# Attention scores in pairs of steps over six PSUM banks, and a transpose moved from TensorE to SyncE

## The chip, the cores and the metric

One core of a Trainium2 chip runs the whole kernel. The metric is the device time of one execution in microseconds, as the median of three runs. Times of single instructions come from one profiled execution of the same program, which is a little shorter than the measured time (612.9 us from its first to its last instruction against 615.9 us).

The engines are TensorE (PE; its weight loads are PEld), VectorE (DVE), ScalarE (ACT), GpSimd (POOL) and SyncE (SP), which here only issues transfers. Each engine runs its own list of instructions in a fixed order, and semaphores hold an instruction until what it needs is there.

## The reference

Eight batches of eight heads, 576 rows, head dimension 64. Attention with a threshold, then a mixer of low rank over the rows, then a two-layer network with relu over the channels:

```python
scores = scale * np.matmul(q, k.transpose(0, 1, 3, 2))          # 64 heads of 576 x 576
thresh = np.max(scores, axis=-1, keepdims=True) - tau
scores = np.where(scores >= thresh, scores, -1000000000.0)
scores = scores - np.max(scores, axis=-1, keepdims=True)
attn = np.exp(scores)
attn = attn / (np.sum(attn, axis=-1, keepdims=True) + 1e-09)
x = np.matmul(attn, v)                                            # heads side by side: (8, 576, 512)

xt = x.transpose(0, 2, 1)
h = xt @ U @ V                                                    # rank 32 over the rows
u = x + h.transpose(0, 2, 1)
ch = np.maximum(u @ w_ch1, 0.0) @ w_ch2                           # 512 -> 2048 -> 512
out = u + ch
```

## The kernel before

The kernel works on head pairs: two heads at a time, 32 pairs in all, four pairs to a batch. A head pair has 4.5 tiles of 128 rows, so two head pairs make nine score steps, and the kernel has 144 of them. A score step computes 128 rows of both heads of a pair against all 576 columns. The head dimension is 64, so TensorE is used as four 64 x 64 tiles: two heads (j) and two halves of the rows (h). All other matmuls use it as one 128 x 128 array. The scores are float32.

```python
pair_bank = [psum.tile([P, 2, 512], FP32, name=f"scores{n}") for n in range(2)]   # 4 banks of PSUM
bank = [psum.tile([P, 512], FP32, name=f"bank{n}") for n in range(4)]             # the other 4

# one score step: 8 matmuls of 64 x 288
for c in range(2):
    cs = slice(c * HC, (c + 1) * HC)
    for j in range(2):
        hs = slice(64 * j, 64 * j + 64)
        for h in range(2):
            a, rows, part = pr, slice(i * P + HB * h, i * P + HB * h + HB), slice(HB * h, HB * h + HB)
            if i == 4:
                a, rows, part = two[h], slice(512, S), two[h].part4
            nc.tensor.matmul(pair_bank[j][part, c, 0:HC], a.tT[hs, 0, rows], a.tT[hs, 1, cs],
                             start=True, stop=True)
```

What follows a score step, for each of the two heads x: VectorE scales the scores out of PSUM and takes the row minimum of the negated scores ("weigh"), ScalarE makes the threshold and the exponential, VectorE selects and sums ("select"), GpSimd copies a piece of the row ("twin"), and SyncE turns the weights by a transposing transfer ("turn_w"; for some of the first pairs TensorE turns them instead, "turn_pe"). Then TensorE multiplies them with the values.

```python
nc.vector.tensor_scalar(out=s_sb.rearrange("p (a c) -> p a c", a=2), in0=pair_bank[x][:, :, 0:HC],
                        scalar1=-scale, scalar2=None, op0=ALU.mult, op1=ALU.min,
                        accum_out=m[:, x:x + 1])                                    # weigh
nc.scalar.activation(out=e_sb, in_=s_sb, func=ACT.Exp, bias=m[:, x:x + 1], scale=-1.0)
nc.vector.scalar_tensor_tensor(out=w_sb[:, 0:S], in0=s_sb, scalar=thr_[:, x:x + 1], in1=e_sb,
                               op0=ALU.is_le, op1=ALU.mult, accum_out=pr.den[:, i, x:x + 1])  # select
nc.sync.dma_start_transpose(...)                                                    # turn_w
```

Later a head pair's u (128 columns of four row tiles) is narrowed to bf16 on ScalarE, turned by four transposes on TensorE into a bank, and copied out by ScalarE:

```python
def turn_u(t):
    ps = bank[t.got[0]][:, 0:256].bitcast(BF16)
    for i in range(4):
        nc.tensor.transpose(ps[:, i * P:(i + 1) * P], pr.ub[:, i, :], identb)

deps = [ub] + (done.get(("p1", pr.b - 2), []) if pr.hp == 0 else [])
uT_ = done["uT_", p] = add(PE, 0.23, turn_u, deps, banks=1, kind="uT")

def copy_u(_):
    nc.scalar.copy(out=bt.uT[:, pr.hp, :], in_=bank[uT_.got[0]][:, 0:256].bitcast(BF16))

done["uT", p] = add(SCA, 0.53, copy_u, [uT_, got("uT", p - 1)], frees=[uT_])
```

The network's first product ("up", 16 groups of four 128x512 matmuls for a batch) is followed by a relu on ScalarE, the second ("down", four quarters of four matmuls each for a row tile) by an addition on VectorE and a store.

The order of all of this is made while the program is built. Each piece of work is a task with an engine, a guessed cost and its dependencies; a list scheduler picks, for each engine, the task with the lowest rank (the guessed time at which it is ready, plus an offset by its kind, OFF). Tasks of the network have due times in score steps (DUE). Where the scheduler expects TensorE idle for more than 0.45 us, it puts in matmuls of the identity with no use but to keep TensorE busy ("fill"). A task that writes PSUM takes the bank that has been free longest:

```python
for e in range(5):
    cands = []
    for t in ready[e]:
        s = max(at[e], t.ready)
        if t.banks:
            s = max(s, last[free[t.banks - 1]])
    ...
    s, t = min((c for c in cands if c[0] <= first + self.PATIENCE[e]), key=rank)
...
while at[PE] + 0.45 < s and last[n] <= at[PE]:
    self.filler(n)
...
t.got = free[:t.banks]
```

Of the kernel before, what the change touches and what calls it, by code (L numbers as in the profile page):

```python
# [8 lines left out]
P = 128  # L9
FP32 = mybir.dt.float32  # L10
# [9 lines left out]
HC = S // 2  # L20
HB = 64
# [3 lines left out]
SOFT = 4  # L25
EARLY = 8


W1_AT = (1, 4, 6, 9, 11, 14, 16, 19)
W2_AT = (20, 21, 23, 24, 25, 26, 28, 29)  # L30

DUE = (218.25, 193.25, 202, 58.75, 370.75, 342.5, 322.25, 741.75)

# [15 lines left out]
class Task:  # L49
    __slots__ = ("engine", "cost", "fn", "deps", "off", "banks", "frees", "lag", "kind", "when",  # L50
                 "dma", "ndma", "steps", "left", "after", "ready", "at", "end", "got")

    def __init__(self, engine, cost, fn, deps=(), banks=0, frees=(), lag=0.0, kind=None,
                 when=None, dma=0.0, ndma=1, steps=0):
        self.engine, self.cost, self.fn = engine, cost, fn
        self.deps = [d for d in deps if d is not None]
        self.banks, self.frees, self.lag, self.kind = banks, frees, lag, kind
        self.steps = steps
        self.dma = dma
        self.ndma = ndma  # L60
        self.when = when
        self.after, self.ready, self.end, self.got = [], 0.0, None, []


class Order:
# [11 lines left out]
    PARTS = {"S": "quadrants"}  # L77


    OFF = {  # L80
        "copy_main": (-65.55, 4.27, -33.19), "copy_rest": (46.32, -22.93, -32.89), "copy_tt":
        (55.52, 75.97, 78.39), "copy_u": (-9.24, 32.51, 27.95), "copy_u4": (-33.7, -103.34, 12.57),
        "copy_w": (26.76, -36.81, 20.04), "down": (9.11, -38.52, 30.41), "exponential": (-75.1,
        348.03, 34.33), "finish": (-81.29, -4.31, -38.11), "first": (-55.84, 39.98, -12.2), "high":
        (318.07, 5.62, 10.21), "inverse": (-108.97, -22.9, -67.36), "join": (10.42, -3.6, 8.15),
        "load": (-8.71, 35.51, -42.16), "low": (12.45, 36.07, 40.66), "low_part": (-39.21, 135.95,
        -5.41), "low_rank": (-33.23, -18.24, 8.92), "make": (-24.27, 38.39, 1.66), "narrow": (-16.4,
        -76.48, 195.67), "narrow_u": (60.65, 3.75, -17.1), "narrow_u4": (-18.43, 20.09, 16.7),
        "norm": (-28.14, -232.63, 8.05), "product": (124.81, 96.76, 14.8), "relu": (108.49, 92.35,
        46.18), "rest": (63.06, -59.16, 27.83), "scores": (-50.96, -12.67, -95.71), "select":  # L90
        (118.77, 57.08, 91.87), "send": (-69.4, 60.79, -21.09), "spread": (48.74, -2.19, -63.39),
        "spread4": (79.29, 25.05, 4.44), "spread_v": (11.62, 75.45, 21.95), "sum_u": (-26.95,
        -36.59, 53.52), "sum_u4": (54.92, -47.81, 31.47), "sums": (-140.25, 32.72, -84.66),
        "threshold": (-37.93, 79.1, -43.59), "turn4": (71.1, 12.6, 27.31), "turn_main": (-113.51,
        69.4, 58.93), "turn_pe": (-18.8, -21.2, 34.54), "turn_rest": (15.16, 27.93, 15.36),
        "turn_u": (-21.99, 92.75, -1.81), "turn_w": (-17.93, -115.14, 3.52), "twin": (-84.09,
        -15.28, -93.69), "up": (-7.21, -32.4, -1.5), "values": (-8.3, -68.34, -10.67), "weigh":
        (28.1, 41.88, 60.36), "weights": (8.1, -7.95, 22.31),
    }
# [4 lines left out]
    def add(self, *args, **kw):  # L104
        t = Task(*args, **kw)
        t.off = self.OFF[t.fn.__name__][self.phase]
        self.tasks.append(t)
        return t

    def run(self):  # L110
# [24 lines left out]
        while left:  # L135
            best = None
            free = sorted(range(self.nbanks), key=lambda n: last[n])
            for e in range(5):
                cands = []
                for t in ready[e]:  # L140
                    s = max(at[e], t.ready)
                    if t.banks:
                        s = max(s, last[free[t.banks - 1]])
                    if e == POOL and t.dma:
                        s = max(s, lanes[t.ndma - 1 - self.LANES])
                    if s < NEVER:
                        cands.append((s, t))
                if not cands:
                    continue
                first = min(s for s, _ in cands)  # L150
                s, t = min((c for c in cands if c[0] <= first + self.PATIENCE[e]), key=rank)
                if best is None or s < best[0]:
                    best = (s, t)
# [15 lines left out]
            left -= 1  # L169
            t.got = free[:t.banks]  # L170
            for n in t.got:
# [13 lines left out]
            for f in t.frees:  # L185
                for n in f.got:
                    last[n] = t.end + self.SIGNAL[e]
# [11 lines left out]
def kernel(  # L199
# [81 lines left out]

    pair_bank = [psum.tile([P, 2, 512], FP32, name=f"scores{n}") for n in range(2)]
    bank = [psum.tile([P, 512], FP32, name=f"bank{n}") for n in range(4)]

# [12 lines left out]
    def got(*key):  # L297
        return done.get(key)
# [73 lines left out]


    def prepare_tasks(p):
        pr = pairs[p]
        loads = load_tasks(p, pr)
# [45 lines left out]


    step = [0]
    tiles = [0]
    gate = {}

    def score_tasks(p, i):


        pr = pairs[p]
        n = step[0]
# [4 lines left out]

        def scores(_):

            for c in range(2):  # L440
                cs = slice(c * HC, (c + 1) * HC)
                for j in range(2):
                    hs = slice(64 * j, 64 * j + 64)
                    for h in range(2):
                        a, rows, part = pr, slice(i * P + HB * h, i * P + HB * h + HB), \
                            slice(HB * h, HB * h + HB)
                        if i == 4:
                            a, rows, part = two[h], slice(512, S), two[h].part4
                        nc.tensor.matmul(pair_bank[j][part, c, 0:HC], a.tT[hs, 0, rows],  # L449
                                         a.tT[hs, 1, cs], start=True, stop=True)  # L450

        deps = [got(name, p + a) for a in range(2 if i == 4 else 1)
                for name in ("qT", "kT", "qk4T")]
        deps += [got("P1", n - 1, x) for x in range(2)]
        S_ = done["S", p, i] = add(PE, 0.97, scores, deps, kind="S", steps=1)
        if i == 4:
            done["S", p + 1, 4] = S_

        mins = []
        for x in range(2):  # L460
            def weigh(_, x=x, s_sb=s_ring[(tiles[0] + x) % NS]):
                nc.vector.tensor_scalar(  # L462
                    out=s_sb.rearrange("p (a c) -> p a c", a=2), in0=pair_bank[x][:, :, 0:HC],
                    scalar1=-scale, scalar2=None, op0=ALU.mult, op1=ALU.min,
                    accum_out=m[:, x:x + 1])

            t = add(VEC, 0.69, weigh, [S_, got("w", tiles[0] + x - NS)])
            done["P1", n, x] = t
            if x == 0 and n in gate:
                for w in gate[n]:  # L470
                    w.deps.append(t)
            mins.append(t)
# [81 lines left out]

    def value_tasks(p):
        pr = pairs[p]
        bt = pr.batch
# [127 lines left out]

        def turn_u(t):

            ps = bank[t.got[0]][:, 0:256].bitcast(BF16)
            for i in range(4):
                nc.tensor.transpose(ps[:, i * P:(i + 1) * P], pr.ub[:, i, :], identb)  # L690

        deps = [ub] + (done.get(("p1", pr.b - 2), []) if pr.hp == 0 else [])
        uT_ = done["uT_", p] = add(PE, 0.23, turn_u, deps, banks=1, kind="uT")

        def copy_u(_):
            nc.scalar.copy(out=bt.uT[:, pr.hp, :], in_=bank[uT_.got[0]][:, 0:256].bitcast(BF16))

        done["uT", p] = add(SCA, 0.53, copy_u, [uT_, got("uT", p - 1)], frees=[uT_])


# [39 lines left out]

    def mixer_tasks(b):
        bt = batches[b]

# [42 lines left out]
        for i in range(NT if bt.odd else 4):  # L786
            halves = []
            for g in range(4):
# [6 lines left out]

                when = due + 134.5 if i == 4 and b < B - 1 else due + 46.5 + 13.25 * (i + g / 4) / 4
                halves.append(add(PE, 0.865, down, (relus4 if i == 4 else relus) + weights2 + (
# [80 lines left out]
    for p in range(0, NP, 2):  # L878
        order.phase = 0 if p < NPAIR else 1 if p < NP - NPAIR else 2
        prepare_tasks(p)  # L880
        prepare_tasks(p + 1)
        for i in range(NT):
            score_tasks(p, i)
        for i in range(4):
            score_tasks(p + 1, i)
        value_tasks(p)
        value_tasks(p + 1)
        if (p + 1) % NPAIR == NPAIR - 1:
            mixer_tasks(p // NPAIR)
# [37 lines left out]
```

## Time and profile before

| | |
|---|---|
| time, median of 3 | 615.9 us (615.58 to 616.2) |
| span of the profiled execution | 612.9 us |
| VectorE, select / weigh | 288 x 861 ns / 288 x 748 ns |
| ScalarE, exponential / relu of "up" | 288 x 772 ns / 144 x 592 ns |
| DMA, mean over the span | 143 GB/s; 87.35 MB |
| granted clock of TensorE | 0.999 |

How to read it: a row of a group names the line, the engine, the operation, what it writes and reads, and how often; then the busy time in us and the mean length of one in ns; then the idle time of the engine just before these instructions and what ended it. Lengths of matmuls are modelled and overlap, so the time that a matmul costs TensorE is read from the starts in the timeline. A row of waits names who waited, for whom, how long in all, how often and the longest.

### The profile page before, as it was taken

The numbers are of one execution on the slowest core, as the hardware profiler recorded it, in microseconds if no ns is written. First come the engines' busy times: TensorE is split into PE (matmuls) and PEld (weight loads), VectorE is DVE, ScalarE is ACT, GpSimd is POOL, SyncE is SP. The second block draws the span as 40 slices with busy tenths as digits, with TensorE's granted clock in tenths as the row PEclk, the third lists the DMA queues.
The fourth block names the chain that finished last, engine by engine and source line by source line (L and its number), as shares of the span: only waits on it lengthen the run. The fifth ranks groups of instructions, "written<-read, shape, count | busy, mean of one in ns | idle before, by whom it ended". The sixth has DMA issues, their size and how long they took to land.

```text
span 612.9 us, 17317 instructions
## 1 busy us (share of the span) xinstructions
PE 600.8 (98%) x6339; PEld 346.1 (56%) x6339; DVE 521.0 (85%) x1399; ACT 478.3 (78%) x983; POOL 361.2 (59%) x596
## 2 busy tenths in 40 slices
PE   7999999999999999999999999999999999999997
PEld 4465655656556555655456655564656655555553
DVE  3999998899999899899976999999998899994201
ACT  4778899988898867997687966998789877984540
POOL 8787768687887656556535755676675732442000
PEclk9999999999999999999999999999999999999999
DMA  7699989987999699977994799889867896464203
GB/s 158 124 167 150 170 152 155 149 157 152 185 163 160 147 174 155 176 146 153 177 157 89 127 182 158 163 135 169 164 129 135 160 196 115 88 126 87 65 13 73
DMA packets 209716, 87.35 MB, mean 143 GB/s; under 512 B 187744, under 2 KB 199984, under 8 KB 209632
## 3 DMA queue, kind: packets, MB, share of 16 engines
q1 hardware_dynamic: 194624, 63.15, 61.2%
q0 software_dynamic: 14048, 22.76, 19.6%
q8 instruction: 50, 0.82, 0.6%
q10 hardware_dynamic: 960, 0.34, 0.2%
q14 instruction: 34, 0.28, 0.2%
HBM read 37.90 MB, written 9.44 MB: 77 GB/s over the span
## 4 chain that ended last, share of the span: by engine, by line
PE 73%; DVE 1%; issue 1%; ACT 0%; DVEq 0%
PE scores L449 19%; PE bank L793 18%; PE bank L760 16%; PE bank L592 9%; PE bank L381 3%; PE bank L776 2%; PE bank L653 1%; PE bank L588 1%; PE bank L668 1%; PE bank L690 1%; PE bank L394 1%; DVE w_ring L489 1%; DVE s_sb L462 0%; PE bank L705 0%; PE bank L727 0%
## 5 line engine op out<-in xcount | busy, mean ns | idle before, releaser
L489 DVE SCALAR_TENSOR_TENSOR w_ring<-s_sb,thr,e_sb 128x576 bf16<-128x576 f32 x288 | 240.0, 861 | 4.5 <-ACT e_sb L482 2.6
L482 ACT ACTIVATE e_sb<-s_sb,m 128x576 bf16<-128x576 f32 x288 | 216.4, 772 | 35.0 <-DVE s_sb L462 34.4
L462 DVE TENSOR_SCALAR_CACHE_REDUCE s_sb<-scores 128x576 f32<-128x576 f32 x288 | 206.6, 748 | 28.5 <-PE scores L449 27.3
L449 PE MATMUL scores<-qkT 64*64 64x288 f32 x2304 | 178.3, 415 | 1.3 <-DVE s_sb L462 1.3
L507 POOL COPY w_ring<-w_ring 128x128 bf16<-128x128 bf16 (+1 forms) x168 | 71.1, 430 | 121.2 <-DVE w_ring L489 87.2
L793 PE MATMUL bank<-W2b,R 128*128 128x512 bf16 x576 | 136.9, 379 | 0.0
L760 PE MATMUL bank<-uT,W1b 128*128 128x512 bf16 x512 | 123.0, 380 | 0.0
L449 PEld LDWEIGHTS scores<-qkT 64*64 64x64 f32 x2304 | 77.7, 132 | 71.5 <-DVE s_sb L462 15.9
L750 ACT ACTIVATE R<-bank 128x512 bf16<-128x512 f32 x144 | 83.0, 592 | 19.2 <-PE bank L760 13.6
L326 POOL DMA_DIRECT2D qkraw<-in_q_dram x125 | 82.1, 663 | 13.8 <-PE bank L381 7.5
L640 POOL TENSOR_TENSOR x<-x,rec 128x256 f32<-128x256 f32 (+1 forms) x84 | 57.4, 685 | 52.4 <-DVE x L633 41.3
L793 PEld LDWEIGHTS <-R 128*128 128x128 bf16 x576 | 53.3, 98 | 57.2 <-issue 5.7
L326 POOL DMA_DIRECT2D qkraw<-in_k_dram x125 | 81.2, 654 | 2.8 <-issue 2.0
L760 PEld LDWEIGHTS <-W1b 128*128 128x128 bf16 x512 | 45.9, 98 | 53.4 <-issue 10.1
L416 POOL TENSOR_TENSOR vh<-vraw_ring,vh 128x512 bf16<-128x512 f32 x64 | 58.5, 914 | 11.7 <-ACT vh L409 8.8
L592 PE MATMUL bank<-vh,wT_ring 128*128 128x128 bf16 x896 | 64.3, 219 | 0.0
L592 PEld LDWEIGHTS <-wT_ring 128*128 128x128 bf16 x896 | 55.5, 98 | 7.6 <-issue 4.4
L805 DVE TENSOR_TENSOR o<-bank,x 128x512 f32<-128x512 f32 x36 | 24.7, 687 | 38.2 <-issue 19.6
L588 PE MATMUL bank<-vh,wT_ring 128*128 128x64 bf16 x256 | 49.3, 193 | 0.3 <-POOL vh L416 0.3
L387 ACT COPY qkT<-bank 128x512 f32<-128x512 f32 x64 | 35.5, 586 | 12.2 <-PE bank L381 11.9
L475 ACT ACTIVATE thr<-m,tau_t 128x2 f32<-128x2 f32 x144 | 42.1, 292 | 3.6 <-DVE s_sb L462 2.9
L381 PE MATMUL bank<-ident,qkraw 128*128 128x128 f32 x256 | 35.6, 275 | 0.0
(72 smaller groups left out, 592.1 us busy)
## 6 DMA issues: line engine op xcount, KB each, us to landing
out_dram<-o SPq DMA_DIRECT2D x71, 128.0 KB, 2.7
vraw_ring<-in_v_dram SPq DMA_DIRECT2D x32, 160.0 KB, 4.0
qkraw<-in_k_dram POOLq DMA_DIRECT2D x63, 80.0 KB, 3.8
qkraw<-in_q_dram POOLq DMA_DIRECT2D x62, 80.0 KB, 4.3
vraw_ring<-in_v_dram SPq DMA_DIRECT2D x32, 128.0 KB, 4.0
qkraw<-in_q_dram POOLq DMA_DIRECT2D x63, 64.0 KB, 4.1
qkraw<-in_k_dram POOLq DMA_DIRECT2D x62, 64.0 KB, 3.9
W1b<-in_moe_w_ch_dram POOLq DMA_DIRECT2D x8, 256.0 KB, 5.3
```

Source lines behind the costliest of these rows:

```text
L326: queue.dma_start(pr.qkraw[part, to, j, :], src[:, j, of, :])
L416: nc.gpsimd.tensor_tensor(out=pr.vh[part, tiles_, :, h, :], in0=raw[part, tiles_], in1=pr.vh[part, tiles_, :, 0, :], op=ALU.subtract)
L449: nc.tensor.matmul(pair_bank[j][part, c, 0:HC], a.tT[hs, 0, rows], a.tT[hs, 1, cs], start=True, stop=True)
L462: nc.vector.tensor_scalar(out=s_sb.rearrange("p (a c) -> p a c", a=2), in0=pair_bank[x][:, :, 0:HC], scalar1=-scale, scalar2=None, op0=ALU ...
L482: nc.scalar.activation(out=e_sb, in_=s_sb, func=ACT.Exp, bias=m[:, x:x + 1], scale=-1.0)
L489: nc.vector.scalar_tensor_tensor(out=w_sb[:, 0:S], in0=s_sb, scalar=thr_[:, x:x + 1], in1=e_sb, op0=ALU.is_le, op1=ALU.mult, accum_out=pr. ...
L507: nc.gpsimd.tensor_copy(out=w_sb[:, xs, S:640], in_=w_sb[:, xs, 512:S])
L592: nc.tensor.matmul(av[:, 2 * a + j, :], w, pr.vh[:, kt, j, :, :], start=kt == 0, stop=False)
L640: nc.gpsimd.tensor_tensor(out=x, in0=x, in1=over_sum(part), op=ALU.mult)
L750: nc.scalar.activation(out=R2[:, fts, lo:hi], in_=bank[t.got[0]].rearrange("p (f c) -> p f c", c=hi - lo), func=ACT.Relu)
L760: nc.tensor.matmul(bank[t.got[0]], W1b[:, dt, ft * P:(ft + 1) * P], bt.uT[:, dt, :], start=(dt == 0), stop=(dt == 3))
L793: nc.tensor.matmul(ch, R2[:, ft, lo:lo + P], W2b[:, ft, :], start=(ft == 0), stop=(ft == 15))
```

## The change

Three things change together.

First, from the third head pair on, score steps are made two at a time. The two score tiles of four banks become two of three banks each ("trio"), one for each head of the pair. The first step of a double lies at columns 224 to 800, the second at 800 to 1376, so both have a part in the middle bank, and each matmul stays inside one bank: 288 and 288 columns for the first, 224 and 352 for the second. Of each nine steps the first stays alone and eight make four doubles. The purpose is to change between the four small tiles and the whole array less often. The six banks of the trios are also given to the other work while no score step needs them (`bank` has eight entries now, six of them in the trios); a horizon (HOLD) keeps them free when a score step is near.

Second, u is turned by a transposing transfer that SyncE issues. The four transposes on TensorE and the copy on ScalarE go.

Third, the offsets are kept for nine phases of the program instead of three, and they and the due times are new, as is the rule for the quarters of "down".

```diff
+PHASES = (1, 2, 3, 4, 5, 6, 8, 28)
+LONE = 2
-DUE = (218.25, 193.25, 202, 58.75, 370.75, 342.5, 322.25, 741.75)
+DUE = (223.75, 153.25, 305, 187.25, 475, 139.5, 104, 429.75)
 ...
+    HOLD = (19.68, 13.12, 21.77, 25.5, 8.99, 31.19, 5.71, 0.33, 42.13)
+    KEPT = ((), (0, 1, 3, 4), (0, 1, 2, 3, 4, 5))
     OFF = {                                  # three offsets a kind become nine
 ...
+            kept = self.KEPT[max([t.trios for t in ready[PE] if t.ready <= at[PE] + self.HOLD[t.phase]],
+                                 default=0)]
+            pool = [n for n in range(self.nbanks) if n not in kept]
+            soonest = min(last[n] for n in pool)
 ...
                     if t.banks:
-                        s = max(s, last[free[t.banks - 1]])
+                        s = max(s, soonest)
+                    if t.trios:
+                        s = max([s] + [last[n] for n in self.KEPT[t.trios]])
 ...
-            t.got = free[:t.banks]
+            if t.trios:
+                t.got = list(self.KEPT[t.trios])
+            elif t.banks:
+                t.got = [min((n for n in pool if last[n] <= max(s, soonest)),
+                             key=lambda n: (n < 6, n % 3 < 2, last[n]))]
 ...
-    pair_bank = [psum.tile([P, 2, 512], FP32, name=f"scores{n}") for n in range(2)]
-    bank = [psum.tile([P, 512], FP32, name=f"bank{n}") for n in range(4)]
+    trio = [psum.tile([P, 1536], FP32, name=f"trio{n}") for n in range(2)]
+    bank = [trio[n // 3][:, n % 3 * 512:(n % 3 + 1) * 512] for n in range(6)] + \
+        [psum.tile([P, 512], FP32, name=f"bank{n}") for n in range(6, 8)]
+    PIECES = (((0, HC), (HC, S)), ((0, 224), (224, S)))
 ...
+        def scores(_):
+            for slot, (p, i) in enumerate(steps):
+                pr, two = pairs[p], pairs[p:p + 2]
+                for piece in range(2):
+                    for j in range(2):
+                        hs = slice(64 * j, 64 * j + 64)
+                        cols = score_cols(slot, j)
+                        lo, hi = PIECES[slot][piece]
+                        for h in range(2):
+                            ...
+                            mm = nc.tensor.matmul(cols[part, lo:hi], a.tT[hs, 0, rows],
+                                                  a.tT[hs, 1, lo:hi], start=True, stop=True)
 ...
+    def score_cols(slot, j):
+        return trio[j][:, 224 + slot * S:224 + (slot + 1) * S]
 ...
                 nc.vector.tensor_scalar(
-                    out=s_sb.rearrange("p (a c) -> p a c", a=2), in0=pair_bank[x][:, :, 0:HC],
+                    out=s_sb, in0=score_cols(slot, x),
 ...
-        def turn_u(t):
-            ps = bank[t.got[0]][:, 0:256].bitcast(BF16)
-            for i in range(4):
-                nc.tensor.transpose(ps[:, i * P:(i + 1) * P], pr.ub[:, i, :], identb)
-        deps = [ub] + (done.get(("p1", pr.b - 2), []) if pr.hp == 0 else [])
-        uT_ = done["uT_", p] = add(PE, 0.23, turn_u, deps, banks=1, kind="uT")
-        def copy_u(_):
-            nc.scalar.copy(out=bt.uT[:, pr.hp, :], in_=bank[uT_.got[0]][:, 0:256].bitcast(BF16))
-        done["uT", p] = add(SCA, 0.53, copy_u, [uT_, got("uT", p - 1)], frees=[uT_])
+        def turn_u(_):
+            nc.sync.dma_start_transpose(
+                bt.uT[:, pr.hp, :].rearrange("p (t r) -> p t r", t=4),
+                pr.ub.rearrange("p t c -> p (t c)"))
+        done["uT_", p] = done["uT", p] = add(
+            SP, 1.3, turn_u, [ub] + (done.get(("p1", pr.b - 2), []) if pr.hp == 0 else []), dma=0.9)
 ...
-                when = due + 134.5 if i == 4 and b < B - 1 else due + 46.5 + 13.25 * (i + g / 4) / 4
+                when = due + 134.5 if i == 4 and b < B - 1 else due + 46.5 + 13.25 * i / 4 - g / 64
 ...
-        for i in range(NT):
-            score_tasks(p, i)
-        for i in range(4):
-            score_tasks(p + 1, i)
+        nine = [(p, i) for i in range(NT)] + [(p + 1, i) for i in range(4)]
+        n = 0
+        while n < 9:
+            two = p >= LONE and n
+            score_tasks(*nine[n:n + (2 if two else 1)])
+            n += 2 if two else 1
```

## The prediction

> **What bounds the kernel now.** I read the page's busy shares first, then the waits of TensorE alone, then the groups of instructions with their forms kept apart, then a stretch of TensorE's timeline in the middle, and last a table of stretches for the DMA.
>
> ```profile
> PE 600.8 (98%) x6339; PEld 346.1 (56%) x6339; DVE 521.0 (85%) x1399; ACT 478.3 (78%) x983; POOL 361.2 (59%) x596
> ```
>
> 98% alone proves nothing, since ends of matmuls are modelled. The waits of TensorE settle it:
>
> ```profile
> PE bank L289 <- DVE identb L224: 3.3, 1, 3.3
> PE scores L449 <- DVE s_sb L462: 1.3, 3, 0.6
> PE bank L520 <- DVE x L617: 0.8, 1, 0.8
> PE bank L596 <- DMA wT_ring<-w_ring: 0.7, 1, 0.7
> PE bank L394 <- DMA qkraw<-in_k_dram: 0.6, 1, 0.6
> ```
>
> Apart from the start (3.3 us) TensorE waits about 4 us in 612.9. It is fed all the time, and the time is what its instruction stream takes from start to start. So I count slots, not busy time. The timeline of TensorE around 300 us gives them (columns: start, length, engine, line, operation):
>
> ```profile
> 299.73 0.38 PE L793 MATMUL bank<-W2b,R 128*128 128x512 bf16 x1
> 300.04 1.20 PE L449 MATMUL scores<-qkT 64*64 64x288 f32 x16
> 301.17 0.33 PE L394 MATMUL bank<-ident,qkraw 128*128 128x128 f32 x1
> 301.34 1.03 PE L793 MATMUL bank<-W2b,R 128*128 128x512 bf16 x4
> 302.20 0.60 PE L381 MATMUL bank<-ident,qkraw 128*128 128x128 f32 x4
> ...
> 309.95 0.40 PE L690 MATMUL bank<-identb,ub 128*128 128x128 bf16 x4
> 310.18 0.39 PE L592 MATMUL bank<-vh,wT_ring 128*128 128x128 bf16 x4
> ```
>
> Four 128x512 matmuls: 302.20 - 301.34 = 0.86, so 0.215 us each. A score step (16 records, 8 instructions): 301.17 - 300.04 = 1.13 us to the next kind. Before it, the matmul that began at 299.73 needs 0.215, so could have been followed at 299.945; the score step starts at 300.04, 0.09 later. Over the whole trace the medians are 1.133 us and 0.093 us. Looking at single starts in this stint, its four rounds of four records begin at 0, 293, 535 and 778 ns, and the next kind 353 ns after the last. A further round inside a stint costs 0.242 us; going in, the first round's extra and going out cost 0.093 + 0.051 + 0.111 = 0.255 us. That is the price of one change of tile mode and back. Four u transposes take 310.18 - 309.95 = 0.23, that is 56 ns each.
>
> The groups that the change touches:
>
> ```profile
> L449 PE MATMUL scores<-qkT 64*64 64x288 f32 x2304 | 178.3, 415 | 1.3 <-DVE s_sb L462 1.3
> L289 PE MATMUL bank<-identb 128*128 128x512 bf16 x78 | 22.2, 408 | 3.3 <-DVE identb L224 3.3
> L696 ACT COPY uT<-bank 128x512 bf16<-128x512 bf16 x32 | 18.5, 579 | 5.0 <-PE bank L690 4.8
> L690 PE MATMUL bank<-identb,ub 128*128 128x128 bf16 x128 | 12.5, 220 | 0.2 <-ACT ub L682 0.2
> ```
>
> The 12.5 us of L690 is union of modelled lengths, of the 56 ns slots only 128 x 0.056 = 7.2 us. L289 are fills: matmuls of the identity that the scheduler places where it expects TensorE idle for over 0.45 us.
>
> Last, the stretches (columns: stretch, busy time and instructions of the five engines in the order PE, PEld, DVE, ACT, POOL, clock, DMA share, GB/s):
>
> ```profile
> 50.00:100.00 50.00, 48.42 (x626) 29.34 (x621) 48.16 (x135) 44.06 (x89) 37.37 (x63) 1.00 0.98 157
> 100.00:150.00 50.00, 49.94 (x558) 30.35 (x551) 46.11 (x125) 44.97 (x93) 38.97 (x68) 1.00 0.93 152
> 150.00:250.00 100.00, 98.96 (x1075) 57.41 (x1074) 95.37 (x256) 84.78 (x180) 70.66 (x114) 1.00 0.96 163
> 250.00:350.00 100.00, 100.00 (x1053) 58.20 (x1051) 87.60 (x233) 81.77 (x170) 56.22 (x96) 1.00 0.81 144
> 350.00:450.00 100.00, 100.00 (x1055) 57.33 (x1053) 96.42 (x259) 81.39 (x171) 63.90 (x102) 1.00 0.93 162
> ```
>
> To see here: DMA is the runner-up, at 0.93 to 0.98 up to 250 us and about 0.87 after, and it keeps up. The clock is full, so no part of the time is throttling.
>
> **What the Trainium skill says.** (1) TensorEngine Tiling (Array Packing), Key Properties: changing the tile mode drains TensorE. The trace agrees: 64*64 to 128*128 and back costs the 0.255 us above. (2) TensorE: Matmul & The Clock Gate, "Wait — 56ns, not 53.3ns?": start to start 55.6 ns at 128 columns and 215.7 at 512. The trace has 56 and 216. (3) PSUM — Partial Sum Buffer, "PSUM bank collisions raise a hardware error": two engines must not be in one bank and quadrant at once, so guard by bank. Both halves of a double score step lie in the middle bank, so the first half can't be read while the second is written; in the program as built the first read waits for the last matmul of its three banks. No run here shows a collision. (4) DMA: Bandwidth & Descriptors, "Issuing engines are not separate DMA queues": all transfers run on the same 16 DMA engines. So a transpose on SyncE's queue takes from the share in the table above.
>
> **The change, part by part.**
>
> Double score steps. In the built program TensorE has 144 separate score stints before; after, 60 doubles of 16 instructions and 24 singles of 8. The columns are the same (288 + 288 + 224 + 352 = 4 x 288). Each double saves one entry and exit: 60 x 0.255 = 15.3 us, all on TensorE's path. A double should last 1.133 + 4 x 0.242 = 2.10 us.
>
> u turned by SyncE. 128 transposes leave TensorE: -7.2 us. ScalarE loses 18.5 us of copies, off the path. SyncE gains 32 transposes of 128x512. The weights' transposes are 120 of 1280 columns and 23 of 640, 168,320 rows of 256 bytes; in the trace such packets take 291 us of 16 engines. 32 x 512 = 16,384 rows more are 28 us more of DMA, from 501 (82% of 613) to 529. Over a span near 594 that is 89% on average.
>
> Fills. 78 become 94: 16 x 0.216 = +3.5 us. They stand where the new order expects idle time (ten each at two places between score steps 23 and 26), so they are planned waiting.
>
> New ranks, due times, nine phases for three. They add no work and move it: from score step 36 on, nine steps carry 8.7 to 17.3 us of the mixer's products (11.2 to 20.0 before), and 55 us of them stay for the end (53 before), counted along the built orders.
>
> VectorE and GpSimd: the same instructions, the score read 128x576 from PSUM contiguous instead of in two pieces; 748 ns before, I expect the same.
>
> Sum on TensorE: -15.3 - 7.2 + 3.5 = -19.0 us. 615.9 - 19.0 = 596.9 if the waits stay as they are.
>
> **Rivals.**
>
> (A) PSUM banks become the wait. A double needs all six banks of the trios empty, and the scheduler keeps them free ahead of it; the other work then has two banks, where before it had four. Laying the slots above along both built orders, after an up-projection stint the bank is written again after 2.8 us (median) and 2.2 us (shortest tenth) before, 2.5 and 1.5 after; after the low-rank product 1.1 becomes 0.65 in the shortest tenth. The relu that empties takes 592 ns and queues behind an exponential of 772, so 1.5 us is about where TensorE begins to wait. I expect 2 to 5 us of it; at worst 12, and 608 us.
>
> (B) The DMA becomes the bound in the first 250 us. There the share is 0.955; transposes are about 0.53 of it. With 9.8% more of them and 2.5% less time: (0.53 x 1.098 + 0.425) / 0.975 = 1.03. Taken literally, 200 us lose 6 us of the gain: 603. Against it: 50 to 100 us already ran at 0.98 with few waits, the packets' time stretches under load, and the new order can move prefetches. I give it 2 us on average.
>
> (C) Bunching: four score tiles land at once, 1 us later than the first did. VectorE then reads four times 0.68 us, ScalarE waits for the first. But VectorE is at 85% and has selects of the previous step to do; with 521 us in 594 it goes to 88%. If order in VectorE doesn't fit the chip, TensorE waits for VectorE before the next double. Each 0.1 us per double is 6 us.
>
> (D) Better than the sum: score stints before have a mean of 1.174 against the median 1.133, 5.9 us of stalls at a second bank's wait; fewer stints may halve that: 593.
>
> **Range and chances.** 596.9, plus 3 for A, 2 for B, 0.5 for C, minus 3.5 for D and a plan that was searched anew for this layout: 599. I take 598.5. The 2% line is 603.6. The saving of 22.5 us of slots is nearly certain, being counted, and needs 10 us of new waits to miss it. Low end 591 (D in full, no new waits), high end 607 (A or B in full). Faster 0.82, within 2% 0.15, slower 0.03.
>
> **What would show it.** Score stints: 60 of about 2.1 us and 24 of 1.13. No u transposes in TensorE's list except the 16 of the batch ends; 32 DMA transposes into uT. TensorE's sum of waits: under 10 us is my sum, 10 to 20 with releasers ScalarE's relu or copies is A, with releasers qkraw or wT_ring transfers is B, score matmuls waiting for VectorE's s_sb is C. DMA share over 0.97 up to 250 us with TensorE idle there would be B. I am wrong if a double takes nearly twice a single, for then the price lies in the steps and not in the mode change, or if waits of over 15 us appear.

## The result, and the profile after

The changed kernel takes 665.8 us (median of 4, 664.4 to 668.6) against 616.05 us: a ratio of 1.081, 95% interval 1.077 to 1.085. It was meant to be faster, I predicted 598.5, and it is 50 us slower. The views come in the same order as for before. The busy shares after:

```profile
PE 602.1 (90%) x6227; PEld 353.5 (53%) x6227; DVE 534.6 (80%) x1399; ACT 461.7 (69%) x951; POOL 375.5 (56%) x596
```

TensorE has 112 instructions fewer and its share has fallen from 98% to 90%: it has less to do and stands still more. Its waits after (who waited, for whom, us in all, times, longest):

```profile
PE trio L339 <- DVE s_sb L528: 12.0, 11, 1.9
PE trio L661 <- DVE s_sb L528: 4.6, 8, 1.3
PE trio L823 <- DVE s_sb L528: 4.1, 7, 0.9
PE trio L722 <- DVE s_sb L528: 3.5, 5, 1.9
...
PE trio L435 <- DVE s_sb L528: 3.3, 8, 0.8
PE bank L448 <- DMA qkraw<-in_k_dram: 3.1, 2, 2.6
```

The rows of this view come to 55.8 us without the start (the 3.3 us before TensorE's first matmul); before, they came to 3.9, the longest 1.3. Now matmuls of every kind (fills L339, attention products L661, up L823, low rank L722, transposes L435) wait for one line: L528, "weigh", VectorE's read of the scores. What they write lies in a trio. Even the fills cost time here: they are of no use, but TensorE's list is in a fixed order, so a fill that waits holds up what stands behind it.

TensorE's timeline around 300 us has the slots (start, length, engine, line, operation):

```profile
297.62 0.39 PE L737 MATMUL bank<-tt,Vb 128*128 128x128 bf16 x4
297.94 2.17 PE L500 MATMUL trio<-qkT 64*64 64x288 f32 x32
300.04 0.33 PE L448 MATMUL bank<-ident,qkraw 128*128 128x128 f32 x1
300.21 0.60 PE L435 MATMUL bank<-ident,qkraw 128*128 128x128 f32 x4
300.97 0.66 PE L435 MATMUL trio<-ident,qkraw 128*128 128x128 f32 x4 [0.16 <-DVE s_sb L528]
```

A double: 300.04 - 297.94 = 2.10 us. Over the trace, 60 doubles have a median of 2.103 us and 24 singles one of 1.133. The last row waits again for L528. The groups and the new transfer (the first row is from before, the others from after; the transfer's row: instructions, median us from issue to landing):

```profile
L462 DVE TENSOR_SCALAR_CACHE_REDUCE s_sb<-scores 128x576 f32<-128x576 f32 x288 | 206.6, 748 | 28.5 <-PE scores L449 27.3
...
L500 PE MATMUL trio<-qkT 64*64 64x288 f32 (+2 forms) x2304 | 165.2, 412 | 2.1 <-DVE x L702 1.7
L528 DVE TENSOR_SCALAR_CACHE_REDUCE s_sb<-trio 128x576 f32<-128x576 f32 x288 | 207.4, 752 | 60.0 <-PE trio L500 31.6
L339 PE MATMUL trio<-identb 128*128 128x512 bf16 x88 | 26.0, 431 | 17.6 <-DVE s_sb L528 12.0
...
uT<-ub SPq DMA_TRANSPOSE x32, 4.1
```

VectorE's read lasts what it did (752 ns against 748), but VectorE stands idle 60.0 us ahead of it, where before it was 28.5. The same stretches as before (busy time and instructions of PE, PEld, DVE, ACT, POOL; clock, DMA share, GB/s):

```profile
50.00:100.00 50.00, 39.74 (x591) 26.98 (x586) 42.72 (x114) 35.68 (x73) 32.82 (x53) 0.93 1.06 143
100.00:150.00 50.00, 44.52 (x427) 25.48 (x417) 37.32 (x101) 38.88 (x78) 30.08 (x54) 0.97 0.81 129
150.00:250.00 100.00, 91.77 (x1010) 56.77 (x1010) 88.17 (x233) 74.91 (x159) 69.39 (x109) 0.98 0.83 150
250.00:350.00 100.00, 92.59 (x943) 53.75 (x942) 92.90 (x239) 73.07 (x153) 59.74 (x93) 1.00 0.97 161
350.00:450.00 100.00, 92.10 (x978) 54.52 (x976) 85.06 (x223) 73.11 (x154) 63.43 (x97) 1.00 0.80 148
```

The loss is in every stretch: TensorE is 8% idle even from 350 to 450 us, where the DMA is at 0.80. In the first 100 us there is something more: DMA at 1.06, and a clock of 0.93. (The DMA share adds up the times of packets, and packets that overlap take it above 1. The 0.93 is a mean: the trace has full clock there but for 6.8 us at half of it, from 83.4 us on; in the 3.4 us ahead of that, TensorE was busy for 1.35.)

To give the whole gap a name I add up, along TensorE's starts, each distance to the next start less the slot (216 ns for 128x512, 56 for 128x128 bf16, 0.093 us more on the way into a score stint, and so on), wherever more than 40 ns are left over, and put it down to what released the later instruction. Below, "slot excess" is this sum:

| releaser, us | before | after |
|---|---|---|
| VectorE emptying PSUM | 3.4 | 51.0 |
| ScalarE emptying PSUM | 0.2 | 8.6 |
| input from ScalarE | 0.7 | 6.7 |
| DMA | 1.8 | 7.7 |
| GpSimd, or none seen | 4.2 | 8.9 |
| all | 10.3 | 82.9 |

It closes. The predicted 596.9 less the 3.0 us between time and span is 593.9; plus 82.9 - 10.3 is 666.5, and the span is 666.9. So the work fell by what I had counted, and 72.6 us of new waiting came. (For the runs below, with their own numbers of fills, it closes to within 4 us.) The question is what is waited for.

### The profile page after: what moved, and what is told of

Read it like the earlier page. It is cut to its first block, busy times and chain, and to the rows that moved or that the text cites. A ratio compares the mean times of both kernels' runs of the same rounds, so it can differ in the third digit from the quotient of the medians.

```text
span 666.9 us, 17014 instructions
## 1 busy us (share of the span) xinstructions
PE 602.1 (90%) x6227; PEld 353.5 (53%) x6227; DVE 534.6 (80%) x1399; ACT 461.7 (69%) x951; POOL 375.5 (56%) x596
## 5 line engine op out<-in xcount | busy, mean ns | idle before, releaser
L528 DVE TENSOR_SCALAR_CACHE_REDUCE s_sb<-trio 128x576 f32<-128x576 f32 x288 | 207.4, 752 | 60.0 <-PE trio L500 31.6
L500 PE MATMUL trio<-qkT 64*64 64x288 f32 (+2 forms) x2304 | 165.2, 412 | 2.1 <-DVE x L702 1.7
L856 PE MATMUL bank<-W2b,R 128*128 128x512 bf16 x496 | 118.3, 379 | 1.8 <-DVE x L702 1.0
L500 PEld LDWEIGHTS trio<-qkT 64*64 64x64 f32 x2304 | 84.7, 133 | 63.4 <-issue 13.0
L823 PE MATMUL bank<-uT,W1b 128*128 128x512 bf16 x368 | 89.8, 379 | 4.5 <-DVE x L702 2.2
L470 POOL TENSOR_TENSOR vh<-vraw_ring,vh 128x512 bf16<-128x512 f32 x64 | 70.4, 1100 | 36.9 <-ACT vh L463 26.6
L823 PEld LDWEIGHTS <-W1b 128*128 128x128 bf16 x512 | 47.2, 98 | 66.7 <-issue 20.2
L813 ACT ACTIVATE R<-bank 128x512 bf16<-128x512 f32 x103 | 59.6, 594 | 11.0 <-PE bank L823 6.3
L661 PEld LDWEIGHTS <-wT_ring 128*128 128x128 bf16 x896 | 56.6, 98 | 14.9 <-issue 9.0
L339 PE MATMUL trio<-identb 128*128 128x512 bf16 x88 | 26.0, 431 | 17.6 <-DVE s_sb L528 12.0
L823 PE MATMUL trio<-uT,W1b 128*128 128x512 bf16 x144 | 36.6, 378 | 5.6 <-DVE s_sb L528 4.1
L661 PE MATMUL bank<-vh,wT_ring 128*128 128x128 bf16 x528 | 38.7, 222 | 1.7 <-DMA wT_ring<-w_ring 1.4
```

The lines of the kernel that those rows point to most:

```text
L470: nc.gpsimd.tensor_tensor(out=pr.vh[part, tiles_, :, h, :], in0=raw[part, tiles_], in1=pr.vh[part, tiles_, :, 0, :], op=ALU.subtract)
L500: mm = nc.tensor.matmul(cols[part, lo:hi], a.tT[hs, 0, rows], a.tT[hs, 1, lo:hi], start=True, stop=True)
L528: nc.vector.tensor_scalar(out=s_sb, in0=score_cols(slot, x), scalar1=-scale, scalar2=None, op0=ALU.mult, op1=ALU.min, accum_out=m[:, x:x + 1])
L661: nc.tensor.matmul(av[:, 2 * a + j, :], w, pr.vh[:, kt, j, :, :], start=kt == 0, stop=False)
L813: nc.scalar.activation(out=R2[:, fts, lo:hi], in_=bank[t.got[0]].rearrange("p (f c) -> p f c", c=hi - lo), func=ACT.Relu)
L823: nc.tensor.matmul(bank[t.got[0]], W1b[:, dt, ft * P:(ft + 1) * P], bt.uT[:, dt, :], start=(dt == 0), stop=(dt == 3))
```

## The experiments

**False sharing (the theory, F).** Look at one such wait in the timeline of after:

```profile
101.77 0.44 PE L588 MATMUL bank<-identb,w_ring 128*128 128x128 bf16 x5 [0.34 <-ACT wT_ring L598]
...
103.28 0.76 DVE L528 TENSOR_SCALAR_CACHE_REDUCE s_sb<-trio 128x576 f32<-128x576 f32 x1
...
103.97 0.08 DVE L528 DVE_READ_ACCUMULATOR s_sb<-trio 128x1 f32 x1
...
104.10 1.44 PE L339 MATMUL trio<-identb 128*128 128x512 bf16 x3 [1.89 <-DVE s_sb L528]
```

The fills at 104.10 write the first bank of trio 0 (bytes 0 to 2047 of a partition). VectorE's read at 103.28 is of the second step of the double, columns 800 to 1376: bytes 3200 to 5503, the second and third bank. They share no bank, and the fills wait 1.89 us. Theory F says that in the built program a wait is held for the whole PSUM tile. A trio is one tile of three banks, so eight banks would behave like four buffers. It goes the other way too (the first row is from before, the others from after):

```profile
DVE s_sb L462 <- PE scores L449: 27.3, 30, 7.4
...
DVE s_sb L528 <- PE trio L500: 31.6, 27, 9.1
...
DVE s_sb L528 <- PE trio L657: 12.4, 14, 1.6
```

VectorE's wait for the scores themselves hardly changed. New is that its score read waits 12.4 us in 14 cases for an attention product that only shares the trio with the scores.

**Run bank_waits.** Nothing moved: the same instructions in the same order on each engine, only what they wait for.

```diff
     ... (shortened; the last line of the kernel, after the order is built)
+    trio_waits_by_bank(nc, tc)
     # for each instruction i that touches a trio:
+    #   wait for the last writer and readers of the *same banks* on other engines (tc.add_manual_dep)
+    #   drop the wait for others of the same trio (tc.declare_no_dep), unless they share another tile with i
```

> The changed kernel with the same instructions in the same order on every engine; only the waits on the two trios follow the bank that is read or written and no longer the whole three-bank tile. Theory F (false sharing: a trio is one tile, so a matmul into its third bank waits for VectorE's reads of the other two, and VectorE's score read waits for a product that TensorE wrote into a bank it does not read): TensorE's waits fall from about 68 us to 15 to 25, time 605 to 625. Rival R1 (SyncE's u transposes hold up the weights' transposes behind them) and rival R2 (the new order itself doesn't fit the chip): still above 650, waits move to other releasers.

Measured: 630.2 us (627.5 to 635.6), ratio 1.022 (1.016 to 1.028). 36 of the 50 us are gone with no instruction moved, so F holds. The time is 5 us above its expectation, and TensorE's waits come to 29.6 us without the start, not to 15 to 25, so F isn't the whole. VectorE's score read now waits for the score matmuls alone (18.6 us); the rows with other products are gone. A second look on another chip, bank_waits_again:

> The kernel with waits by bank once more, beside the one that turns a quarter of u on the same chip, so that the two can be compared: 628 to 633.

Measured: 629.6 us (626.9 to 631.9), 1.022 (1.017 to 1.027). The same place in its timeline:

```profile
98.38 0.44 PE L644 MATMUL bank<-identb,w_ring 128*128 128x128 bf16 x5 [0.33 <-ACT wT_ring L654]
...
98.76 0.74 DVE L584 TENSOR_SCALAR_CACHE_REDUCE s_sb<-trio 128x576 f32<-128x576 f32 x1
...
98.89 2.33 PE L395 MATMUL trio<-identb 128*128 128x512 bf16 x10
```

The ten fills (L395 here) now follow after 0.51 us instead of 2.33, and while they run VectorE goes on reading other banks of the trios.

**Run before_paired.** The converse: the kernel before, with its order and single steps, and its four work banks declared as two tiles of two banks.

```diff
-    bank = [psum.tile([P, 512], FP32, name=f"bank{n}") for n in range(4)]
+    duo = [psum.tile([P, 1024], FP32, name=f"duo{n}") for n in range(2)]
+    bank = [duo[n // 2][:, n % 2 * 512:(n % 2 + 1) * 512] for n in range(4)]
```

> The kernel before, the same order, with its four work banks allocated as two tiles of two banks instead of four of one. Nothing else. F: a matmul into one bank now waits for the emptying of its neighbour, slower by 15 to 60 us (630 to 675). R1 and R2: no change, 616.

Measured: 680.5 us (679.4 to 681.7), 1.102 (1.099 to 1.106): 64 us, a little over the expected range, for two lines of allocation. TensorE's waits there:

```profile
PE duo L794 <- DVE x L634: 4.1, 8, 0.9
PE duo L761 <- ACT R L751: 3.6, 7, 1.2
...
PE duo L593 <- ACT qkT L388: 2.9, 5, 0.9
PE duo L654 <- ACT R L751: 2.3, 4, 0.7
```

To see: up (L761), the low-rank product (L654) and others wait for relus (L751), additions and copies. In before, in the same order and with a tile for each bank, none of these rows is there. The slot excess is 73.1 us, 37.1 of it ScalarE emptying and 23.0 VectorE. So waits by tile cost time in the old order too.

**Run u_on_pe.** The rival R1: SyncE's transfer of u is to blame, through its queue. After, with u turned on TensorE and copied by ScalarE as before (the scheduler orders around it anew, and puts in 31 fills more).

```diff
-            nc.sync.dma_start_transpose(bt.uT[:, pr.hp, :]..., pr.ub...)
+            for i in range(4):
+                nc.tensor.transpose(ps[:, i * P:(i + 1) * P], pr.ub[:, i, :], identb)
+            # and copy_u on ScalarE
```

> The changed kernel with u turned on TensorE and copied by ScalarE as before; doubles, trios and new offsets stay. R1: SyncE's queue is free again, faster by 40 us or more (below 626). F: 128 transposes of 56 ns come back and the false waits stay, within 15 us of the changed kernel (650 to 680).

Measured: 680.7 us (678.7 to 681.2), 1.103 (1.099 to 1.107). It is 15 us worse, not better; R1 falls. Of the 15, 7.2 are the transposes and 31 x 0.216 = 6.7 the fills; the slot excess is 80.9 us against 82.9. So the sum of the waiting doesn't hang on who turns u. Its parts shift: in this order TensorE's waits for transfers are 1.7 us instead of 6.7, while its excess for ScalarE emptying PSUM rises from 8.6 to about 16.

**Run before_u_sync.** The other half alone: before's single steps, banks and offsets, u turned by SyncE.

> The kernel before with only u turned by SyncE's transfer, old offsets, order made anew for it. R1: slower by 20 us or more (above 636). F and R2: TensorE loses 7.2 us of slots and the order is not tuned for it, 608 to 622.

Measured: 632.2 us (630.1 to 636.3), 1.025 (1.020 to 1.030), between what R1 (above 636) and F (608 to 622) expected. 7.2 us of transposes are gone, but the new order has 103 fills for 78, which takes 25 x 0.216 = 5.4 us of that back. The slot excess is 30.2 us against 10.3; of it wT_ring transfers 6.1 and qkraw transfers 4.4. Whether that is the transfers or an order that no longer fits, this run can't tell; the last pair says more.

**Run u_quarter.** Theory D (not the prediction's rival D): u's rows fill the DMA in the first part. bank_waits, with only one of u's four row tiles turned. The other three parts of uT are zeros from the start, so the mixer's products read zeros there; all instructions on the engines stay, save two of VectorE that write the zeros. 12,288 of 16,384 rows go, 21 us of packets by the prediction's 1.7 ns a row.

```diff
-                bt.uT[:, pr.hp, :].rearrange("p (t r) -> p t r", t=4),
-                pr.ub.rearrange("p t c -> p (t c)"))
+                bt.uT[:, pr.hp, 0:P], pr.ub[:, 0, :])
```

> The kernel of the run with waits by bank, the same order, but SyncE's transfer turns only one of the four column tiles of u (128 of 512 rows of 256 bytes); the other three quarters of the turned u stay zero, so the network's product isn't the reference's. It leaves out 24 of the 32 x 512 = 16,384 rows in thousandths terms: 12,288 rows, about 21 us of the 16 DMA engines, and nothing else. Theory D (what is left after the false waits is the DMA, full up to 300 us): TensorE's waits for q, k and weight transfers fall from some 19 us to under 8, time 612 to 622. Rival P (what is left is idle time planned into the new order): 627 to 633, as with the whole transposes.

Measured: 631.9 us (630.4 to 633.2), 1.025 (1.022 to 1.028), against 629.6 for bank_waits_again on the same chip. The 2.2 us more are the start, where TensorE waits 5.5 us instead of 3.3 until VectorE has written the zeros. The waits for transfers were to fall under 8 us; they come to 15.8, against 13.6 in bank_waits_again. The longest rows of u_quarter:

```profile
PE trio L397 <- DVE identb L326: 5.5, 1, 5.5
...
PE bank L506 <- DMA qkraw<-in_k_dram: 4.6, 3, 2.4
```

Nothing is gained, so D falls. The packets of the whole run take 21 us less, as counted, but the DMA share from 15 to 110 us is 1.03 with and without these rows: they are not what fills the DMA there.

**Run weights_part.** Theory D2: it is the weights of the network, fetched from 15 to 110 us, that crowd the DMA. bank_waits, with one eighth of W1's columns and half of W2's rows fetched (about 26 us of packets less were expected; the trace has 521 us in all for 549); the up and down products read the fetched part again instead of the rest, in as many matmuls of the same shape.

```diff
             cs = slice(h * (F // 2), (h + 1) * (F // 2))
+            cs = slice(h * (F // 2), h * (F // 2) + 128)
 ...
-                W2b[:, 2 * c:2 * c + 2, :],
-                moe_w_ch2[2 * c * P:(2 * c + 2) * P, :].rearrange("(c p) m -> p c m", p=P))
+                W2b[:, 2 * c, :], moe_w_ch2[2 * c * P:(2 * c + 1) * P, :])
 ...
-                    nc.tensor.matmul(bank[t.got[0]], W1b[:, dt, ft * P:(ft + 1) * P],
+                    nc.tensor.matmul(bank[t.got[0]], W1b[:, dt, ft // 8 * 1024:ft // 8 * 1024 + P],
 ...
-                        nc.tensor.matmul(ch, R2[:, ft, lo:lo + P], W2b[:, ft, :],
+                        nc.tensor.matmul(ch, R2[:, ft, lo:lo + P], W2b[:, ft // 2 * 2, :],
```

> The kernel with waits by bank, the same order and the same number of instructions, but each of the eight loads of the first weight matrix fetches 128 of 1024 columns and each of the eight loads of the second fetches one of its two row blocks, and the matmuls read only what was fetched. The result isn't the reference's; all sizes and waits of the matmuls stay. It leaves out about 26 us of DMA between 15 and 110 us. Theory D2 (the DMA is full in the first 110 us because the weights come in beside transposes and q, k loads; that is what is left there): TensorE's waits for transfers in the first 110 us fall from 13 us to under 4 and the time to 614 to 622. Rival P2 (the transfers are late because SyncE and GpSimd issue them late in the new order): waits of 10 us or more stay, 626 to 632.

Measured: 620.1 us (617.7 to 622.2), 1.0055 (1.0037 to 1.0073): 9.5 us less than bank_waits_again, on another chip (13.3 us above before there, 4.3 here). The waits of TensorE for the inputs, first bank_waits:

```profile
PE bank L491 <- DMA qkraw<-in_q_dram: 5.0, 3, 3.7
PE bank L504 <- DMA qkraw<-in_k_dram: 4.8, 3, 2.6
```

and weights_part:

```profile
PE bank L504 <- DMA qkraw<-in_k_dram: 2.3, 2, 1.5
...
PE bank L491 <- DMA qkraw<-in_q_dram: 1.2, 1, 1.2
```

In the first 110 us, excess put down to DMA is 13.4 us in bank_waits_again and 5.6 here: the time is as D2 expected, the waits fell less far than its "under 4". The stretches, first bank_waits_again:

```profile
50.00:100.00 50.00, 40.96 (x560) 26.50 (x558) 43.62 (x114) 35.61 (x73) 33.22 (x52) 0.93 1.02 137
100.00:150.00 50.00, 48.35 (x492) 28.45 (x492) 42.74 (x117) 42.73 (x86) 35.19 (x63) 1.00 0.96 155
```

and weights_part:

```profile
50.00:100.00 50.00, 42.58 (x594) 27.52 (x595) 47.97 (x130) 39.70 (x80) 35.01 (x59) 1.00 0.91 133
100.00:150.00 50.00, 48.83 (x521) 29.63 (x520) 42.95 (x116) 42.32 (x86) 36.92 (x65) 1.00 0.75 133
```

The DMA share falls from 1.02 to 0.91, and the clock rises from 0.93 to 1.00 as well. The granted clock over the span, median of the runs, is 0.9915 in bank_waits_again and 0.997 in weights_part; times 630, that is 3.5 us. So of the 9.5 us some 6 are waits for transfers and up to 3.5 the clock. What sets the clock was not tried.

**Runs new_ranks and u_sync_ranks.** Is what remains the banks, or an order that doesn't fit? Both have u turned by SyncE and offsets, due times and horizons searched anew, with transfers taken 6% longer; new_ranks has doubles and waits by bank, u_sync_ranks before's single steps and banks. Edits: only the numbers of OFF, DUE and HOLD against bank_waits and before_u_sync.

> Double score steps, u turned by SyncE and waits by bank, with offsets, due times and horizon searched anew so that the order also holds if transfers take 6% longer than the scheduler guesses. If the order's tightness against late transfers is what is left (theory D2 seen from the other side), TensorE's waits for transfers fall from 15 us to under 10, time 612 to 624. If the true waits for banks are what is left (theory A), they stay at about 15 us and the time at 624 to 632.

> The kernel before with single score steps and its own banks, u turned by SyncE, offsets and due times searched anew in the same way. TensorE has 7.2 us of slots fewer than before and no false waits; beside the run with the old offsets (632) it tells what a fitting order is worth. 612 to 624; under 616 it would beat the kernel before.

Measured: new_ranks 628.9 us (624.9 to 630.9), 1.019 (1.014 to 1.024). u_sync_ranks 618.6 us (617.2 to 622.3), 1.0042 (1.0025 to 1.0060). TensorE's longest waits in new_ranks:

```profile
PE bank L721 <- DMA wT<-w_ring: 5.1, 2, 3.2
PE bank L491 <- DMA qkraw<-in_q_dram: 4.2, 3, 2.3
```

and in u_sync_ranks, past the start:

```profile
PE bank L422 <- DMA qkraw<-in_k_dram: 2.9, 2, 1.7
PE bank L548 <- POOL w_ring L535: 2.5, 2, 2.2
```

A new order gave before_u_sync 13.5 us back (632.2 to 618.6), so most of that run's loss goes with the order. Whether the new one gains because it fits the new list of work or because it allows for late transfers isn't parted. That order runs at a DMA share above 1 and waits 3.5 us for transfers in all. Its stretch from 50 to 100 us:

```profile
50.00:100.00 50.00, 44.40 (x567) 26.67 (x567) 45.05 (x127) 37.73 (x76) 34.04 (x56) 0.97 1.09 153
```

A new order gave bank_waits nothing that can be told from the spread, and its waits for transfers, which were to fall under 10 us, stayed at 14.2. Between the two, doubles cost 10 us where their slots should save 15.3. Slot excess is 45.5 us in new_ranks and 16.1 in u_sync_ranks: PSUM still being emptied 14.2 against 4.1, inputs from ScalarE 7.0 against 0.7, DMA 16.1 against 4.6. No version here beats the kernel before. Doubles with u on TensorE and waits by bank were not run.

## Why the prediction was wrong

The steps of the sum that held:
- Price of a mode change: 2.10 us for a double was expected, 2.103 measured, 60 of them. The 15.3 us are saved.
- u off TensorE: 7.2 us, gone. Fills: 94, as counted. VectorE's read: same length, as expected.
- The packets of u: 529 us of all packets were expected (501 before), 531 measured.
- The closure above: 593.9 plus new waits gives the span to within a microsecond. So -19.0 us is what the work does.

The step that failed is "596.9 if the waits stay as they are", and behind it rival A, "PSUM banks become the wait ... I expect 2 to 5 us of it; at worst 12". A named the right place, PSUM: TensorE's excess for banks being emptied rose from 3.6 to 59.6 us, more than ten times what I expected. But its reason was wrong for most of it. I looked for two banks emptied too late by ScalarE's relus and copies; ScalarE is 8.6 us of the 59.6, and 51.0 are VectorE, mostly score reads that hold up matmuls of every other kind. There are two parts.

First, and largest: I followed reuse bank by bank through both orders. The built program waits tile by tile, and the change makes six banks into two tiles. I even wrote that "the first read waits for the last matmul of its three banks", put it down to the middle bank that a double's halves share, and didn't ask what else that waiting covers. It is 36 us of the gap (bank_waits), and 64 when done to before (before_paired). The page on PSUM that I leaned on (the Trainium skill, PSUM — Partial Sum Buffer, "PSUM bank collisions raise a hardware error") speaks of the same bank and quadrant, and says that accesses to different banks run clean; so those waits guard nothing that the chip asks for. bank_waits agrees: it does without them and is 36 us faster than after. I read from the page what the chip demands and took it for what the program waits for.

Second, with the false waits gone, 15.4 us of excess for PSUM remain in bank_waits_again (10.6 VectorE, 4.8 ScalarE) where before had 3.6. That is rival A proper, about 12 us more, its worst case. It is read from the trace; no run takes these waits away by themselves, since there is no ninth bank to give.

Rival B, transfers. I gave 2 us, with 6 as its literal value, and spread it over 250 us. It came in the first 110: weights_part returns 9.5 us, up to 3.5 of them the clock. And u's rows, on which B was built, are not the cause by their bulk: leaving three quarters out gave nothing. before ran at 0.98 from 50 to 100 us with hardly a wait, and I took that as a sign that there was room. It was no such sign, and the 1.03 that I worked out was no bound either: u_sync_ranks ran at 1.09 there with 3.5 us of waits for transfers in the whole span, bank_waits_again at 1.02 with 13.6.

Rival C, VectorE late because four score tiles land at once, does not stand out by itself: score matmuls (L500) wait 1.7 us in 3 cases in after, the longest row of theirs. Rival D went the other way: what score stints last beyond their medians was 6.0 us before and is 15.3 after (singles 1.41 us in the mean, doubles 2.25).

The gap of 68.9 us from 596.9 to 665.8 so: 36 false waits (run); about 6 waits for early transfers and up to 3.5 of clock (run, the split by the clock's records); about 12 true waits for banks and 6 inputs from ScalarE (7.1 against 0.7), both read from bank_waits_again against before. That is some 64. The other 5 are waits for later transfers and what had no releaser in the trace; the experiments don't part them. How much of the last 18 a better order could take back is open: one search of new ranks took none.

The range failed with the sum: I had called 10 us of new waits the margin, and named "waits of over 15 us" as what would make me wrong. By the view of waits they are 55.8, by slot excess 72.6 more than before.

## What to carry to other kernels

Before you share a PSUM tile of several banks out to other work, look at what the built program waits for: if it waits by tile, give each bank a tile of its own, or state the waits by bank, for then a tile of n banks acts as one buffer. Where TensorE is 98% busy in an order searched for it, slots saved are sure and small (19 us here), and a change of buffers can cost several times that (72.6 us of waiting here); follow the waits of the built program, not only its slots. And a transfer share near 1 doesn't tell what the waits will be: here 0.98 and 1.09 went with few and 1.02 with many, each in its own order.

## What the runs showed that I had not expected

Two lines of allocation, with every instruction the same, are worth 64 us of 616 (before_paired). The granted clock differs between kernels and between runs of one kernel: 0.990 to 0.997 over after's four runs, whose times go with it (668.6 us at 0.990, 664.4 at 0.997: 0.7% of 665 is 4.7). In before_paired, with nearly as much waiting but none over 1.4 us past the start, it is 0.998 to 1.000, so waiting alone doesn't lower it; nor did one wait of 2.6 us in weights_part (0.999). What does was not tried.
